# Another PSUM bank for the second token tile's inner values, and output products two steps behind

## The chip, the cores and the metric

The kernel runs on one core of one Trainium2 chip. The time is that of one execution on the device, in microseconds (us). Three runs of the kernel before took 954.71 to 959.58 us, with a median of 956.01.

## The reference

Inputs are q, k and v of 4 batches, 8 heads, 576 positions and 64 values, and two pairs of weights, 512 x 2048 and 2048 x 512. Everything is float32.

```
scores = q k^T / 8 - slope[h] * |i - j|       where 0 <= i - j < 128, else -1e9
x   = softmax(scores) v                        (2304 tokens x 512)
h   = x @ w_in;   g = h * clip(h + 3, 0, 6) / 6;   x = g @ w_out       (layer 1)
h   = x @ w_in2;  g = s * relu(h)^2 + b;           out = g @ w_out2    (layer 2)
```

## The kernel before, in words

**Precision.** Each float32 factor is split into a high half (rounded to fp32r) and a low half (the rest), and a product is made of three matmuls: high x high, high x low, low x high. So x, g and the weights all exist as two halves.

**Tiles and steps.** Layer 1 has eight token tiles (t = 0 to 7): four of 256 tokens, then four of 320. Layer 2 has six of 384 tokens (t = 8 to 13). The 2048 inner values are 16 blocks f of 128. A step (t, f) consists of: an inner product `h` (L563, 12 matmuls into one PSUM bank), `relu` on ScalarE (ACT, L580), `product` on VectorE (DVE, L586), `hi` on ACT, which writes the high half of g (L596), `lo` on DVE, which writes the low half (L605), and an output product `o` on TensorE (PE, L615), which adds the block's share to the tile's output banks. In layer 1 the product reads the PSUM bank of h again; in layer 2 only relu reads it. After a tile's last step, `end` (L651) copies the output banks out, in turn on ACT and DVE, and stores them: layer 1 to a buffer in DRAM, `x2d`, from which layer 2 loads its input, layer 2 to the output. Tile 7 writes its result into one SBUF buffer `whole` (L655) with the tag that x of tile 7 had before, and two transfers on SyncE (SP) take it from there.

**Order.** The whole program is written out by hand. Each piece of work is put into a numbered slot with a rank (`at`, L69), and the slots are emitted in order, within a slot by rank. Each engine runs its own instructions strictly in that order. A step i of the list `steps` has h in slot 14 + 2i (one earlier for t = 2 to 6), relu and product in the same slot, hi and lo in the next, and o in the slot `oslot + 1`. With the `oslot` of L82, PE's order is h of step i+1, o of step i, h of step i+2, o of step i+1. In the list the steps of tiles 0 and 1 alternate, tile 1 four blocks behind; the other tiles come one after another.

**What else runs beside the steps.** Until about 140 us the weights of layer 1 are split, two halves per block (`Half`, L141): ACT writes a scaled copy z into a PSUM bank and scales the raw words (L177, L178), DVE puts sign and exponent together (L182, L185), POOL adds (L191), ACT writes the high half (L199), and DVE the low half (L203). From tile 7 to the last block of tile 8 the weights of layer 2 are split in the same way; their z lies in the PSUM bank of tag "h". Attention of the token tiles 2 to 7 (`Unit`, L238) runs beside the steps too, one unit of one head every four slots: scores s (PE, L319), minima on DVE (L335, L336), exponentials on ACT (L346), weights on POOL (L362), transposes t (PE, L371), a copy F on ACT (L375), masks on POOL (L387), values v (PE, L402).

**Banks.** PSUM has eight banks. Four (tags o0 to o3) hold outputs. One, of tag "h", holds h of tiles 0 to 6. Three, of tag "a", rotate: s, t, v and the z of layer 1 take them (`bank`, L128), and from tile 7 on h does. A tile with a tag gets the buffer of that tag that has been free longest in program order, and its first instruction waits for the last reader of the tile that had it.

**SBUF buffers of the change.** The late pool has two buffers each of the tags "t" (the activation) and "g" (both halves of g).

Of the kernel before, what the change touches and what calls it, by code (L numbers as in the profile page):

```python
# [9 lines left out]
F32R = mybir.dt.float32r  # L10
# [6 lines left out]
P = 128  # L17
# [5 lines left out]
def tile_alibi_window_attention_moe_moe2(  # L23
# [17 lines left out]
    NF = w1.shape[0]  # L41
# [12 lines left out]
    xpool = ctx.enter_context(tc.tile_pool(name="xpool", bufs=1))  # L54
# [6 lines left out]
    nt1 = len(SIZES1)  # L61
# [10 lines left out]
    FIRST = 14  # L72
# [6 lines left out]
    hslot, oslot = {}, {}  # L79
    for i, tf in enumerate(steps):  # L80
        hslot[tf] = FIRST + 2 * i - 1
        oslot[tf] = FIRST + 2 * i + 2  # L82

# [11 lines left out]
    own = const.tile([P, P], I32, name="own")  # L97
# [43 lines left out]
    class Half:  # L141
# [51 lines left out]
        def hi(self):  # L193
            if (self.layer, self.f) not in wt:
                wt[self.layer, self.f] = wpool.tile(
                    [P, 2, 2 * DM], F32R, tag=f"w{self.f}", name=f"w{self.layer}_{self.f}"
                )
            w = wt[self.layer, self.f]
            nc.scalar.activation(w[:, 0, self.c], self.l.bitcast(F32), AF.Copy)  # L199
# [11 lines left out]
    xtag = ["x0", "x1", "x2"] + [f"x{(i + 1) % 2}" for i in range(3, nt1)]  # L211
    N2R = SIZES1[2]

    def x_tile(i):
        if i not in xt:
            n = N2R if xtag[i] == "x2" else N1
            xt[i] = xpool.tile([P, CC, 2, n], F32R, tag=xtag[i], name=f"x{i}")
            xt[i] = xt[i][:, :, :, : SIZES1[i]]
        return xt[i]
# [18 lines left out]
    class Unit:  # L238


        def __init__(self, g, b, qa, qb, h):
            self.g, self.b, self.qa, self.qb, self.h = g, b, qa, qb, h
            self.ka = max(0, qa - 1)
            self.nq = min(qb * P, S) - qa * P
            self.nk = min(qb * P, S) - self.ka * P
            self.nkb = qb - self.ka
            self.id = f"{b}_{qa}_{h}"
# [173 lines left out]
    class StartUnit(Unit):  # L421
# [111 lines left out]
    raws = {}  # L533
    units = [
        (StartUnit if i < NATIVE else Unit)(i, *g, h)
        for i, g in enumerate(groups)
        for h in range(H)
# [5 lines left out]
    class Step:  # L543
# [19 lines left out]
        def h(self):  # L563
            w = wt[self.layer, self.f]
            x = x_tile(self.t) if self.layer == 1 else xt[self.t]
            tag = dict(tag="h") if self.t < nt1 - 1 else dict(tag="a", bufs=3)
            self.ps = ps_w.tile([P, 512], F32, name=f"h{self.t}_{self.f}", **tag)[:, : self.n]
            m = 0
            for cc in range(CC):
                for wp, xp in ((0, 0), (0, 1), (1, 0)):  # L570
                    nc.tensor.matmul(  # L571
                        self.ps,
                        lhsT=w[:, wp, cc * P : (cc + 1) * P],
                        rhs=x[:, cc, xp],
                        start=m == 0,
                        stop=m == 3 * CC - 1,
                    )
                    m += 1
# [16 lines left out]

        def hi(self):  # L596
            pool, n = (gpool, N1) if self.layer == 1 else (late["p"], N2)
            self.g = pool.tile([P, 2, n], F32R, tag="g", name=f"g{self.t}_{self.f}")
            self.g = self.g[:, :, : self.n]
            if self.layer == 1:  # L600
                nc.scalar.activation(self.g[:, 0], self.a, AF.Copy)  # L601
            else:
                nc.scalar.activation(self.g[:, 0], self.a, AF.Identity, bias=b_sb)  # L603

        def lo(self):  # L605
            hi = self.g[:, 0].bitcast(F32)
            if self.layer == 1:
                nc.vector.tensor_tensor(out=self.g[:, 1], in0=self.a, in1=hi, op=ALU.subtract)  # L608
            else:
                nc.vector.scalar_tensor_tensor(  # L610
                    out=self.g[:, 1], in0=self.a, scalar=b_sb, in1=hi,
                    op0=ALU.add, op1=ALU.subtract,
                )
# [106 lines left out]
    for k in range(2 * NF):  # L720
        f, i = divmod(k, 2)
# [83 lines left out]
```

## Time and profile before

| | |
|---|---|
| median of three runs | 956.01 us (954.71 to 959.58) |
| the profiled execution, its own time | 958.67 us |
| its span, first to last instruction | 956.9 us |
| TensorE busy | 938.5 us, 98% |
| VectorE busy | 532.3 us, 56% |
| ScalarE busy | 465.9 us, 49% |
| GpSimd busy | 270.4 us, 28% |
| DMA, read and written | 63.44 MB and 9.44 MB |
| mean granted clock of TensorE | 0.985 |

The profile is one execution. Busy time counts the instructions of an engine, and a matmul's end is modelled, so a full PE row does not say that PE is at its peak. PEld is TensorE's weight load, which overlaps the matmuls. In a timeline each row is one instruction or a run of equal ones (x12 is twelve): start, duration, engine, line, operation, what it writes and reads, the shapes, and in brackets the idle time of the engine before it with the engine that released it. A row of the waits names who waited for whom: us in total, how often, the longest.

### The profile page before, as it was taken

Reading aid. Unit: us, or ns where it says so; the run is one execution under the profiler, and the core shown is the slowest. Engines: PE = TensorE matmul, PEld = TensorE weight load, DVE = VectorE, ACT = ScalarE, POOL = GpSimd, SP = SyncE. Lnnn points to the kernel's source line nnn. Section 1 sums busy time; section 2 is a strip of 40 time slices with the busy share of each in tenths; the row PEclk is TensorE's granted clock in tenths of the full one; section 3 lists DMA queues with packets and bytes.
Section 4 is the critical chain, followed back from the end, with each engine's and each line's share of the span. In section 5 each row is a group of like instructions: output and inputs, shape, how many; then the busy total and the mean of one; then the engine's idle time right before and its main releaser. Section 6 shows DMA issues by size and latency. Waiting matters only on the chain.

```text
span 956.9 us, 16309 instructions
## 1 busy us (share of the span) xinstructions
PE 938.5 (98%) x5978; PEld 865.6 (90%) x5978; DVE 532.3 (56%) x1334; ACT 465.9 (49%) x1201; POOL 270.4 (28%) x544
## 2 busy tenths in 40 slices
PE   8998999999999999999999999999999999999998
PEld 5688889999999999999999888799999999999997
DVE  5999885555555555455359999733333323323322
ACT  4988885455554545454347767523223223323322
POOL 5535773345544444434104533100000000000000
PEclk7699999999999999999999999999999999999999
DMA  7244632223221121220046455010200200200000
GB/s 286 89 160 140 206 114 75 81 73 105 67 95 61 49 96 61 73 72 17 1 144 193 142 182 165 13 54 1 66 1 1 66 1 1 66 1 0 34 1 34
DMA packets 34383, 73.92 MB, mean 77 GB/s; under 512 B 4352, under 2 KB 13568, under 8 KB 34304
## 3 DMA queue, kind: packets, MB, share of 16 engines
q1 hardware_dynamic: 34304, 72.89, 23.2%
q8 instruction: 47, 0.77, 0.3%
q14 instruction: 32, 0.26, 0.1%
HBM read 63.44 MB, written 9.44 MB: 76 GB/s over the span
## 4 chain that ended last, share of the span: by engine, by line
PE 78%; DVE 9%; ACT 4%; DMA 3%; issue 3%; POOL 1%; SPq 0%; ACTq 0%; POOLq 0%; DVEq 0%
PE h L571 34%; PE o L643 18%; PE o L629 16%; PE s L319 3%; PE v L402 3%; DMA raw<-w 2%; DVE w L203 2%; DVE z L182 2%; PE t L371 2%; PE s L474 2%; ACT z L177 1%; DVE t L592 1%; DVE raw L185 1%; PE t L513 1%; ACT w L199 1%
## 5 line engine op out<-in xcount | busy, mean ns | idle before, releaser
L571 PE MATMUL h<-x,w 128*128 128x384 f32 (+2 forms) x2688 | 445.9, 315 | 4.3 <-DVE t L588 4.2
L571 PEld LDWEIGHTS h<-x,w 128*128 128x128 f32 x2688 | 417.6, 189 | 15.1 <-DVE t L588 6.3
L584 ACT ACTIVATE t<-h 128x384 f32<-128x384 f32 (+2 forms) x224 | 99.5, 444 | 366.7 <-PE h L571 366.6
L629 PE MATMUL o<-g,w 128*128 128x256 f32 (+1 forms) x1536 | 230.4, 299 | 1.7 <-DVE g L608 1.2
L643 PE MATMUL o<-w,g 128*128 128x512 f32 x864 | 216.8, 395 | 3.5 <-ACT g L603 2.0
L629 PEld LDWEIGHTS o<-g,w 128*128 128x128 f32 x1536 | 210.0, 189 | 3.8 <-DVE g L608 1.9
L643 PEld LDWEIGHTS o<-w,g 128*128 128x128 f32 x864 | 159.9, 188 | 36.3 <-ACT g L603 4.5
L592 DVE SCALAR_TENSOR_TENSOR t<-t,s_sb 128x384 f32<-128x384 f32 x96 | 63.1, 658 | 171.5 <-ACT t L584 171.5
L387 POOL TENSOR_SCALAR_AFFINE_SELECT W<-F 128x128 f32<-128x128 f32 (+1 forms) x240 | 68.0, 320 | 148.9 <-ACT F L375 148.8
L588 DVE SCALAR_TENSOR_TENSOR t<-t,h 128x256 f32<-128x256 f32 (+1 forms) x128 | 57.7, 451 | 83.6 <-ACT t L584 83.6
L610 DVE SCALAR_TENSOR_TENSOR g<-t,b_sb,g 128x384 fp32r<-128x384 f32 x96 | 63.7, 663 | 54.1 <-ACT g L603 54.0
L608 DVE TENSOR_TENSOR g<-t,g 128x256 fp32r<-128x256 f32 (+1 forms) x128 | 70.5, 551 | 40.2 <-ACT g L601 39.4
L603 ACT ACTIVATE g<-t,b_sb 128x384 fp32r<-128x384 f32 x96 | 59.2, 617 | 63.6 <-DVE t L592 63.6
L191 POOL TENSOR_TENSOR raw<-raw 128x512 int32<-128x512 int32 x47 | 54.5, 1159 | 106.8 <-DVE raw L185 44.4
L601 ACT ACTIVATE g<-t 128x256 fp32r<-128x256 f32 (+1 forms) x128 | 56.0, 437 | 16.1 <-DVE t L588 16.1
L300 POOL TENSOR_TENSOR C<-raw,C 64x448 fp32r<-64x448 f32 (+1 forms) x48 | 51.0, 1062 | 36.2 <-issue 22.5
L362 POOL TENSOR_SCALAR P<-P,st 128x128 f32<-128x128 f32 x128 | 53.0, 427 | 7.1 <-DVE st L356 5.6
L346 ACT ACTIVATE P<-P,st 128x128 f32<-128x128 f32 x128 | 49.6, 391 | 0.0
L335 DVE COPY_PREDICATED s<-own,s 128x128 f32<-128x128 int32 (+1 forms) x112 | 30.8, 275 | 33.0 <-PE s L319 31.2
L182 DVE TENSOR_SCALAR z<-z 128x512 int32<-128x512 int32 x64 | 44.1, 689 | 1.1 <-ACT z L177 0.7
L203 DVE TENSOR_TENSOR w<-raw,w 128x512 fp32r<-128x512 f32 x47 | 42.6, 907 | 0.0
L336 DVE CUSTOM_DVE_ANT_0 P<-s,rel 128x128 f32<-128x128 f32 x128 | 37.2, 290 | 7.3
(73 smaller groups left out, 778.5 us busy)
## 6 DMA issues: line engine op xcount, KB each, us to landing
raw<-w SPq DMA_DIRECT2D x47, 512.0 KB, 4.3
raw<-qk SPq DMA_DIRECT2D x32, 384.0 KB, 3.0
stage<-w SPq DMA_DIRECT2D x17, 512.0 KB, 5.3
out<-y SPq DMA_DIRECT2D x18, 256.0 KB, 2.3
raw<-qk SPq DMA_DIRECT2D x16, 256.0 KB, 2.6
rv<-v SPq DMA_DIRECT2D x16, 256.0 KB, 3.3
raw<-qkv0p SPq DMA_DIRECT2D x8, 384.0 KB, 7.2
x2d<-y SPq DMA_DIRECT2D x8, 320.0 KB, 2.7
```

What stands on the lines that cost most here:

```text
L182: nc.vector.tensor_scalar(out=z, in0=z, scalar1=3, scalar2=None, op0=ALU.logical_shift_left)
L203: nc.vector.tensor_tensor(out=w[:, 1, self.c], in0=self.l.bitcast(F32), in1=w[:, 0, self.c].bitcast(F32), op=ALU.subtract,)
L387: nc.gpsimd.affine_select(out=self.W[:, o : o + r], in_=self.F[:, q : q + r], fill=0.0, base=k - 1, compare_op=ALU.is_ge, pattern=[[s, r]] ...
L571: nc.tensor.matmul(self.ps, lhsT=w[:, wp, cc * P : (cc + 1) * P], rhs=x[:, cc, xp], start=m == 0, stop=m == 3 * CC - 1,)
L584: nc.scalar.activation(self.a, self.ps, AF.Relu, **bias)
L588: nc.vector.scalar_tensor_tensor(out=self.a, in0=self.a, scalar=6.0, in1=self.ps, op0=ALU.min, op1=ALU.mult)
L592: nc.vector.scalar_tensor_tensor(out=self.a, in0=self.a, scalar=s_sb, in1=self.a, op0=ALU.mult, op1=ALU.mult)
L603: nc.scalar.activation(self.g[:, 0], self.a, AF.Identity, bias=b_sb)
L608: nc.vector.tensor_tensor(out=self.g[:, 1], in0=self.a, in1=hi, op=ALU.subtract)
L610: nc.vector.scalar_tensor_tensor(out=self.g[:, 1], in0=self.a, scalar=b_sb, in1=hi, op0=ALU.add, op1=ALU.subtract,)
L629: nc.tensor.matmul(acc[t][d], lhsT=w[:, wp, DM + d * P : DM + (d + 1) * P], rhs=self.g[:, gp], start=f == 0 and i == 0 and (t > 1 or d % 2 ...
L643: nc.tensor.matmul(acc[t][tb], lhsT=self.g[:, gp, tb * P : (tb + 1) * P], rhs=w[:, wp, DM:], start=f == 0 and i == 0, stop=f == NF - 1 and ...
```

## The change

Three edits. In `Step.h` the inner values of tile 1 take a bank of tag "a" in place of the bank "h". In the list of slots the o of layer 2 comes two slots later, so that PE's order there is h of step i+2, o of step i, h of step i+3, o of step i+1. At the boundary o of tile 7's last step stays where it is, and h of two more steps of tile 8 comes before the first o of tile 8. As a step's g now lives longer, `Step.hi` gives each third g of layer 2, beginning with the first of tile 8, a place in the buffer that held `whole`, the result of tile 7.

```diff
-        oslot[tf] = FIRST + 2 * i + 2
+        oslot[tf] = FIRST + 2 * i + (2 if tf[0] < nt1 else 4)
...
-            tag = dict(tag="h") if self.t < nt1 - 1 else dict(tag="a", bufs=3)
+            own = self.t != 1 and self.t < nt1 - 1
+            tag = dict(tag="h") if own else dict(tag="a", bufs=3)
...
-            self.g = pool.tile([P, 2, n], F32R, tag="g", name=f"g{self.t}_{self.f}")
+            tag = "g"
+            if self.layer == 2 and (self.t * NF + self.f) % 3 == 2:
+                pool, tag = xpool, xtag[nt1 - 1]
+            self.g = pool.tile([P, 2, n], F32R, tag=tag, name=f"g{self.t}_{self.f}")
```

## Rows read from the trace of the kernel before

**Rows 1.** Page, first part: busy us, share of the span, instructions.
```profile
PE 938.5 (98%) x5978; PEld 865.6 (90%) x5978; DVE 532.3 (56%) x1334; ACT 465.9 (49%) x1201; POOL 270.4 (28%) x544
```
**Rows 2.** Waits of PE in the whole span: us, times, longest.
```profile
PE h L571 <- DVE t L588: 4.2, 8, 1.3
```
**Rows 3.** Busy time by stretch: length, each engine's busy time, PEclk, DMA, GB/s.
```profile
72.00:96.00 24.00, 21.52 (x169) 20.11 (x168) 23.28 (x55) 20.36 (x50) 13.62 (x17) 1.00 0.49 144
...
549.00:612.00 63.00, 60.05 (x82) 1.00 0.40 132
```
**Rows 4.** Timeline of PE in layer 2, one step and the next h.
```profile
858.63 2.27 PE L571 MATMUL h<-x,w 128*128 128x384 f32 x12
860.74 2.24 PE L643 MATMUL o<-w,g 128*128 128x512 f32 x9
862.82 2.27 PE L571 MATMUL h<-x,w 128*128 128x384 f32 x12
```
**Rows 5.** Timeline of PE while tiles 0 and 1 alternate.
```profile
87.83 1.70 PE L571 MATMUL h<-x,w 128*128 128x256 f32 x12 [1.26 <-DVE t L588]
...
99.34 1.60 PE L571 MATMUL h<-x,w 128*128 128x256 f32 x12
100.78 0.24 PE L319 MATMUL s<-C,qX 128*128 128x128 f32 x1
...
101.25 1.59 PE L629 MATMUL o<-g,w 128*128 128x256 f32 x12
103.42 1.70 PE L571 MATMUL h<-x,w 128*128 128x256 f32 x12 [0.57 <-DVE t L588]
...
109.22 0.23 PE L319 MATMUL s<-C,qX 128*128 128x128 f32 x1
...
114.53 1.60 PE L571 MATMUL h<-x,w 128*128 128x256 f32 x12
...
119.00 1.70 PE L571 MATMUL h<-x,w 128*128 128x256 f32 x12 [0.58 <-DVE t L588]
```
**Rows 6.** Timelines of ACT and DVE there: readers of rotating banks.
```profile
100.22 0.36 ACT L375 ACTIVATE F<-t 128x256 f32<-128x256 f32 x1
...
109.56 0.69 DVE L185 SCALAR_TENSOR_TENSOR raw<-raw,z 128x512 int32<-128x512 int32 x1
...
113.89 0.64 ACT L177 ACTIVATE z<-raw 128x512 f32<-128x512 f32 x1 [0.69 <-DMA raw<-w]
...
115.80 0.36 ACT L375 ACTIVATE F<-t 128x256 f32<-128x256 f32 x1
```
**Rows 7.** Timelines of ACT, DVE and PE at the start of layer 2.
```profile
548.57 0.62 ACT L603 ACTIVATE g<-t,b_sb 128x384 fp32r<-128x384 f32 x1
...
550.58 0.98 DVE L610 SCALAR_TENSOR_TENSOR g<-t,b_sb,g 128x384 fp32r<-128x384 f32 x1
...
549.24 0.50 PE L643 MATMUL o<-w,g 128*128 128x512 f32 x1
```
**Rows 8.** Timeline of SP, and the landing of line 667's two transfers there.
```profile
550.34 0.81 SPq L667 DMA_DIRECT2D x2d<-y  x2
...
DMA to landing us min/median/max: 2.2/3.0/3.7
```
**Rows 9.** Timelines of DVE and PE, and waits from 543 to 612 us.
```profile
610.30 1.53 DVE L203 TENSOR_TENSOR w<-raw,w 128x512 fp32r<-128x512 f32 x1
...
611.41 2.48 PE L571 MATMUL h<-x,w 128*128 128x384 f32 x12
...
DVE g L610 <- ACT g L603: 2.3, 4, 0.7
...
PEld h L571 <- DVE w L203: 0.3, 1, 0.3
```
**Rows 10.** Timeline of PE's weight loads at the last output product.
```profile
951.42 1.48 PEld L643 LDWEIGHTS o<-w,g 128*128 128x128 f32 x7 [0.36 <-DVE g L610]
```
**Rows 11.** Line 610 from 551 to 612 us: duration in ns, min/median/max.
```profile
L610 DVE SCALAR_TENSOR_TENSOR g<-t,b_sb,g x14: 607/620/1400, 550.6 to 609.8; 128x384 fp32r<-128x384 f32 x14
```

## The prediction

> **What bounds the kernel now.** I read four views in this order. The page's first part: TensorE (PE) is busy for 98% of the span, VectorE (DVE) for 56% [rows 1]. That is a mean over stages, so next the waits: PE stands before an inner product for 4.2 us in eight places, always behind DVE's product, the last reader of the one bank that the first two token tiles share [rows 2]. Then the busy time by stretch: from 72 to 96 us DVE is busy for 23.28 of 24 us, and from 549 to 612 for 60.05 of 63 [rows 3]. In these stretches DVE splits the weights besides its share of the steps, and PE's gaps follow from that. Last the timelines of the two places that the change touches [rows 5 to 9]. Elsewhere PE sets the pace: in the second layer a step is an inner product (h) of 860.74 - 858.63 = 2.11 us and an output product (o) of 862.82 - 860.74 = 2.08 [rows 4].
>
> What the reader should keep: where DVE is full, giving PE room ahead buys nothing unless DVE itself gets faster.
>
> **Part 1: tile 1's h in the rotating banks.** It removes the waits on the shared bank and adds the 16 h of tile 1 to three banks that attention (s, t, v) and weight splitting (z) already use. PE instructions, shapes and order stay the same.
>
> *What goes.* The 4.2 us of [rows 2]. Three of the eight places come after 100 us, 0.57 and twice 0.58 (103.42, 119.00 and the same 15 us later) [rows 5]; so 2.5 us lie before 90 us, the largest 1.26 at 87.83 [rows 5], where DVE has 24 - 23.28 = 0.7 us in 24 to spare [rows 3]. A PE that arrives earlier only stands at the next thing that DVE's work releases: the transposes of attention wait for POOL's weights, which wait for DVE, and that wait grows by what the earlier one loses. Of this stretch I take 0.5 us as gained, as relu and the z copies reach DVE sooner; its ends are 0 and 2.5.
>
> *What comes.* Banks go round in the order in which they fall free in program order. With h of tile 1 put into that order, each tile's start in the trace can be held against the end of the last reader of the bank that it would get. Up to 99 us each is free, or all but free. Then five places are not:
> - h at 99.34 gets the bank whose transposes are copied out at 100.22 + 0.36 = 100.58: 1.24 us late [rows 5, 6].
> - s at 109.22 gets the bank of a z whose last DVE operation ends at 109.56 + 0.69 = 110.25: 1.03 late [rows 5, 6].
> - h at 114.53 gets the bank copied out at 115.80 + 0.36 = 116.16: 1.63 late [rows 5, 6].
> - The last two places come once more 15 us later, the same pattern.
>
> These 1.24 + 2 x (1.03 + 1.63), some 6.6 us, don't add up on the path, because waits that PE has now are eaten by them. Queued behind a waiting h or s on PE are the o of the step before and the next h; ACT's relu waits for them. Step by step: h of 99.34 starts at 100.6, s and o follow, and the h that now starts at 103.42 after 0.57 us of waiting [rows 5] needs no bank any more and starts at 100.6 + 1.44 (h) + 0.47 (s) + 1.44 (o, as h) = 104.0: 0.6 late [rows 5]. ACT gets its relu 0.6 late, so z and its end are too: s of 109.22 starts at 110.9, and all behind it is 1.6 late. The copy at 115.80 comes 1.0 late (ACT has 0.69 of waiting for a load to lose [rows 6]), h of 114.53 starts at 117.2, and the h of 119.00, rid of its 0.58 us of waiting, at 120.6: 1.6 late. So the pair of units costs 1.0 beyond the 0.6, and the next pair 1.0 more: 2.6 us. After 140 us the z are over and PE sets the pace, so a shift stays. Part 1: 2.6 - 0.5 = +2.1. From below: all 4.2 gone and no new wait, -4.2. From above: the full 6.6.
>
> **Part 2: o two steps behind.** A step's o now comes after h of the next two steps. One h is merely moved before each o, so no instruction comes or goes; three g tiles are needed, and each third lies in the space of the buffer that held the last layer-1 result (y of tile 7).
>
> *A new wait at the start.* (8*16 + 0) % 3 is 2: the very first g of the layer is the one in y's space. It can't be written before both transfers of y to DRAM have landed. Now ACT writes that g at 548.57. When DVE has finished y, the two transfers are issued from 550.34 on for 0.81 us and take 2.2 and 3.7 us to land [rows 8]; I take the second as the longer: about 550.75 + 3.7 = 554.45. So g's first half ends at 554.45 + 0.61, and DVE's second half, at 550.58 now [rows 7], starts at 555.1: 4.5 us late, less 0.36 as it then runs beside no POOL work (0.98 against a median of 0.62 [rows 7, 11]): 4.2. Queued behind on ACT: a weight half, the relu of the next step, z; behind on DVE: everything. SP's transfers aren't behind it. With a landing as fast as the first, 2.2 us, it would be 2.7.
>
> *Where does this land on the path?* From 551 to 612 DVE's queue is full: 3 us of 63 idle [rows 3], 2.3 of it the way from product over ACT to the second half inside one step [rows 9], none of it a wait for PE. So a late DVE stays late until the last weight half. Its split for h of step 15 runs 610.30 to 611.83, and h of that step, at 611.41, already waits for it (0.3 us) [rows 9]. After the change it is ready at 611.83 + 4.2 = 616.0. PE's own work allows 607.5: o of step 0 from 555.1 on, then 12 h of 2.11 and 13 o of 2.08. So DVE decides, and PE stands for 8 us in between. The granted clock is 1.00 throughout now [rows 3]; should it fall in the gap of 4 us, PE has those 8 us in hand.
>
> *What is left behind it.* Before, o of step 13 precedes h of step 15; now only o of step 12 does. So one o, 2.08 us, moves from the time in which PE waited for DVE to the time after it. This is so even without the new wait: room for PE to run ahead makes the order of what it can do worse, as h waits for weights and o is the work that could fill the gap.
>
> *What goes.* From 549.24 [rows 7] to 611.41 [rows 9] are 62.2 us for 14 o and 13 h, 29.1 + 27.4 = 56.5: 5.7 us of PE waiting for g. They vanish as waits for g and come back as waits for weights, as above. At the very end the last o no longer stands behind its g: 951.42 shows 0.36 on the weight loads [rows 10]; I take 0.3 off. Part 2: 4.2 + 2.1 - 0.3 = +6.0. From below: no late landing and half of DVE's 3 us of idle time won back, 2.1 - 1.5 - 0.3 = +0.3; or the whole 5.7 gone, if DVE didn't bind, -6. From above: a landing 1 us later, +7. Switches between the tiles of layer 2 show no gap now and keep the same h between two tiles' o.
>
> **Sum.** +2.1 + 6.0 = +8.1 us. The profiled execution took 958.67 us (span 956.9) and would take 966.8. The median of the runs is 956.01, 2.7 below; with it 964.1. I forecast 964.
>
> **Rivals.**
> *A, the shift is made up: 958.* DVE loses time to POOL: a second half of g takes 0.62 us in the median of 14 and up to 1.40 [rows 11], the long ones where they start beside POOL's add. If the 4.2 us of shift takes five such apart, at 0.78 each, DVE is back in time: then part 2 is 2.1 - 0.3, and with part 1 at nothing 956.0 + 1.8 = 957.8. Against: POOL's add is released by DVE's own operation before, so it falls on the same place. The Trainium skill's SBUF — State Buffer (Who interferes with whom) says that the two engines share a port pair, that a DVE instruction with two SBUF inputs meets a POOL one that reads SBUF there, and that the later one is blocked wholly; the trace agrees, with 0.78 us of blocking; were it gone for good, DVE would be A's.
>
> *B, the other side, faster: 946.* Between 551 and 612 PE stops for g; with a second step of room it doesn't stop, and relu reaches ACT and DVE sooner, so that the weights too come sooner. Then 4.2 + 5.7 + 0.3 go, 956.0 - 10.2 = 946. The point from which it decides is whether DVE's full stretch ends before 607.5, when PE's own work reaches h of step 15. For it: the gaps lie exactly where the change gives room. Against: DVE has 3 us idle there, none of it from PE. The Trainium skill's Perfetto Trace Analysis (Optimization Strategy) has the rule on this side: gaps that repeat can mean that there are too few buffers for the next tile; by it the time is B's. Here the gaps stand on an engine that waits for a full one.
>
> *C, more: 970.* The bank waits do add up, since a z without a bank holds the relu behind it on ACT and so takes away the slack that eats them: 956.0 + 6.6 + 7.
>
> *D, only the order of o counts:* no late landing on the path, part 1 as forecast: 956.0 + 2.1 + 1.8 = 959.9.
>
> **How the numbers follow.** Forecast 0.58 (its own range 960 to 968), A 0.13, D 0.14, B 0.08, C 0.07. 0.5% of 956 is 4.8 us, about what a measurement of this kernel can tell from no change; faster means under 951.2, slower over 960.8. Faster is B: 0.08. Same is A and D: 0.27. Slower is the forecast and C: 0.65. The range reaches to A and C and leaves out B and what lies beyond these two: 957 to 970.
>
> **What would show it.** Right, if in the profile after: (1) ACT's first second-layer g starts near 554 behind a transfer, and PE shows one gap of about 4 us there; (2) DVE stays full to about 616, and PE's gaps before that stand on DVE's weight halves at h (few do now); (3) the waits of h for DVE's product before 140 us are gone, and h and s wait for ACT's copy and DVE's sign operation, over a us each, from 99 us on; (4) tile 2 starts about 2 us later. The prediction is wrong if DVE's stretch ends by 612, if the first g doesn't wait, or if the first 160 us come out shorter.

## The result and the profile after

The changed kernel takes 969.68 us (median of 4 runs, 968.26 to 971.32), the one before 957.8 in the runs beside it: a ratio of 1.0115, 95% interval 1.0082 to 1.0148, so 11.0 us more (7.9 to 14.2; the two medians lie 11.9 apart). The profiled execution took 969.79 us with a span of 968.1, which is 11.2 above the span of before.

The first part of the page shows as much work as [rows 1], in a longer span (busy us, share, instructions):

```profile
PE 941.2 (97%) x5978; PEld 870.6 (90%) x5978; DVE 533.0 (55%) x1334; ACT 465.8 (48%) x1201; POOL 267.6 (28%) x544
```

PE has the same 5978 matmuls and yet 2.7 us more busy time: some of them ran slower. Where the time went is best read by holding the start of each inner product against its start in the kernel before. That is a subtraction of two PE timelines, worked out here for after and for four of the experiments below (us, positive is later; "(t, f)" is token tile and step):

| start of h | after | part 1 alone | part 2 alone | part 2, third g in y's space | the same, gaps filled |
|---|---|---|---|---|---|
| (0, 0) | +0.69 | -1.06 | +0.68 | -0.12 | -0.89 |
| (1, 4), about 92 us | +1.87 | -1.34 | +0.66 | +0.45 | -0.94 |
| (1, 11), about 145 us | +4.31 | +1.76 | +1.46 | +0.18 | -1.59 |
| (7, 15), about 540 us | +4.28 | +1.73 | +1.45 | +0.17 | -1.62 |
| (8, 15), about 611 us | +6.09 | +1.71 | +3.22 | -1.52 | -3.27 |
| (13, 15), about 947 us | +9.27 | +1.75 | +6.20 | +2.87 | -1.63 |
| span | +11.2 | +1.8 | +7.9 | +4.6 | +0.1 |

Three things are to be seen. From 145 to 540 us the numbers stand still, in all of them: there PE sets the pace. Before that they drift even where layer 1 is as it was: by +0.8, +0.3 and -0.7 us from (0, 0) to (1, 11) in the last three columns, and by +1.3 and +3.0 in two runs further down, the second of which began 6.7 us early. So a shift of less than about 1 us in the first 145 us needn't come from a change. And where part 2 is in, the span grows by some 1.7 us more than the last h: the o of 2.08 that is left over at the end, less 0.3 or so of the old tail.

**The first 160 us.** PE's own waits between 36 and 160 us, the three largest sums (us, times, longest):

```profile
PE h L572 <- ACT F L375: 3.1, 3, 1.0
PE s L319 <- DVE raw L185: 2.2, 3, 0.9
PE t L371 <- POOL P L362: 2.1, 2, 1.7
```

The 4.2 us of h behind DVE's product [rows 2] are gone from this list (0.5 us is left, at 61 us, for tile 0). In their place h waits for ACT's copy F of a transpose, and s for the DVE operation that ends the life of a z. The places, on PE's timeline:

```profile
101.77 1.69 PE L572 MATMUL h<-x,w 128*128 128x256 f32 x12 [1.04 <-ACT F L375]
...
112.04 0.30 PE L319 MATMUL s<-C,qX 128*128 128x128 f32 x1 [0.85 <-DVE raw L185]
...
118.30 1.69 PE L572 MATMUL h<-x,w 128*128 128x256 f32 x12 [1.04 <-ACT F L375]
```

These are the h of 99.34, the s of 109.22 and the h of 114.53 in [rows 5], now 2.4, 2.8 and 3.8 us later. Three shorter waits for a z's DVE operation are new too: s at 78.22 and at 85.18 us, 0.52 each, and h at 142.89, 0.44. And PE is already 1.87 us late before the first of the three rows, at (1, 4); 0.69 of that was there at the first h. At (1, 3), 83 us, it was 0.09 late, so 0.6 had been won; then 1.8 were lost at a place that the prediction named for its wait, but not for the clock. After, and then the same two transposes before:

```profile
87.14 1.60 PE L572 MATMUL h<-x,w 128*128 128x256 f32 x12
90.44 0.33 PE L371 MATMUL t<-ident,P 128*128 128x128 f32 x1 [1.70 <-POOL P L362]
91.21 0.48 PE L371 MATMUL t<-ident,P 128*128 128x128 f32 x1 [0.45 <-POOL P L362]
91.34 2.91 PE L633 MATMUL o<-g,w 128*128 128x256 f32 x12
94.05 1.70 PE L572 MATMUL h<-x,w 128*128 128x256 f32 x12
```

```profile
89.80 0.33 PE L371 MATMUL t<-ident,P 128*128 128x128 f32 x1 [0.27 <-POOL P L362]
90.57 0.33 PE L371 MATMUL t<-ident,P 128*128 128x128 f32 x1 [0.45 <-POOL P L362]
```

Before, h of 87.83 waited 1.26 us for DVE [rows 5] and the transposes 0.27 and 0.45. Now h is early, and the transposes behind it wait 1.70 and 0.45 us for POOL's weights. The o after them takes 2.91 us, at a granted clock of 0.50 from 91 to 93 us; an o of this shape takes 1.59 [rows 5].

**The start of layer 2.** Timeline of all engines from 553.5 us:

```profile
554.63 0.80 SPq L671 DMA_DIRECT2D x2d<-y  x2
...
558.04 0.61 ACT L607 ACTIVATE g<-t,b_sb 128x384 fp32r<-128x384 f32 x1 [5.20 <-DMA x2d<-y]
...
558.68 0.62 DVE L614 SCALAR_TENSOR_TENSOR g<-t,b_sb,g 128x384 fp32r<-128x384 f32 x1 [3.73 <-ACT g L607]
558.70 3.79 PE L647 MATMUL o<-w,g 128*128 128x512 f32 x9 [3.17 <-ACT g L607]
```

The first g waits for y's two transfers, as forecast. Against [rows 7] DVE's second half is 558.68 - 550.58 = 8.10 us late; 4.31 of that came with it from the first 160 us, so 3.8 are new; as the operation takes 0.62 us now and took 0.98, 3.4 are left behind it. PE's gap there is 3.17 us, and its first o takes 3.79 instead of 2.24 us [rows 4]. In the stretches by time (length, busy time of PE, PEld, DVE, ACT and POOL, granted clock, DMA share, GB/s) the clock falls behind that gap, and once more after 616 us:

```profile
553.00:560.00 7.00, 3.83 (x18) 3.32 (x17) 3.23 (x7) 1.96 (x4) 1.04 (x1) 0.89 0.49 170
560.00:563.00 3.00, 3.00 (x11) 2.43 (x11) 2.97 (x5) 3.00 (x7) 0.97 (x1) 0.68 0.52 171
...
616.00:626.00 10.00, 7.03 (x27) 6.27 (x28) 6.48 (x10) 3.97 (x7) 1.19 (x1) 0.83 0.00 0
```

**The end of DVE's full stretch.** DVE's split for h of step (8, 15), then PE's timeline from 611 us:

```profile
618.00 1.53 DVE L203 TENSOR_TENSOR w<-raw,w 128x512 fp32r<-128x512 f32 x1
```

```profile
611.20 2.03 PE L572 MATMUL h<-x,w 128*128 128x384 f32 x10 [1.42 <-DVE w L203]
613.07 2.25 PE L647 MATMUL o<-w,g 128*128 128x512 f32 x9
617.49 0.61 PE L572 MATMUL h<-x,w 128*128 128x384 f32 x2 [2.17 <-ACT w L199]
619.58 3.30 PE L572 MATMUL h<-x,w 128*128 128x384 f32 x10 [1.47 <-DVE w L203]
622.67 2.56 PE L647 MATMUL o<-w,g 128*128 128x512 f32 x9
625.07 2.27 PE L572 MATMUL h<-x,w 128*128 128x384 f32 x12
```

DVE's operation starts 7.70 us later than in [rows 9], 3.4 beyond the 4.31. PE has done all it may do and stands before h's first and third matmul. Behind these two gaps ten matmuls of h take 3.30 us (2.03 in the step before, the first row) and o 2.56 (2.25): 1.6 us lost to the slow clock (a mean of 0.83 from 616 to 626 us, in the stretches above), with nothing in hand.

### The profile page after: what moved, and what is told of

It is laid out like the page before. It is cut to its first block, busy times and chain, and to the rows that moved or that the text cites. A ratio compares the mean times of both kernels' runs of the same rounds, so it can differ in the third digit from the quotient of the medians.

```text
span 968.1 us, 16322 instructions
## 1 busy us (share of the span) xinstructions
PE 941.2 (97%) x5978; PEld 870.6 (90%) x5978; DVE 533.0 (55%) x1334; ACT 465.8 (48%) x1201; POOL 267.6 (28%) x544
## 4 chain that ended last, share of the span: by engine, by line
PE 80%; DVE 10%; ACT 4%; issue 3%; DMA 1%; POOL 0%; SPq 0%; ACTq 0%; POOLq 0%; DVEq 0%
PE h L572 35%; PE o L647 18%; PE o L633 17%; PE s L319 3%; DVE w L203 3%; PE v L402 2%; DVE z L182 2%; PE s L474 2%; PE t L371 2%; DVE raw L185 1%; DVE t L593 1%; ACT z L177 1%; PE t L513 1%; DVE g L612 1%; DVE t L589 1%
## 5 line engine op out<-in xcount | busy, mean ns | idle before, releaser
L647 PEld LDWEIGHTS o<-w,g 128*128 128x128 f32 x864 | 162.1, 189 | 34.2 <-ACT g L607 4.5
L362 POOL TENSOR_SCALAR P<-P,st 128x128 f32<-128x128 f32 x128 | 50.6, 410 | 7.0 <-DVE st L356 5.5
```

The costliest lines, as they stand in the source:

```text
L647: nc.tensor.matmul(acc[t][tb], lhsT=self.g[:, gp, tb * P : (tb + 1) * P], rhs=w[:, wp, DM:], start=f == 0 and i == 0, stop=f == NF - 1 and ...
```

## The experiments

In all of them the kernel before ran on the same chip. A difference in us is the ratio of the times, less 1, by some 959 us. Two parts, and what hangs on each, come first; then the causes in part 2; last the early steps of part 1.

### Part 1 alone

```
-            tag = dict(tag="h") if self.t < nt1 - 1 else dict(tag="a", bufs=3)
+            own = self.t != 1 and self.t < nt1 - 1
+            tag = dict(tag="h") if own else dict(tag="a", bufs=3)
```

> Part 1 alone: h of tile 1 in the rotating banks, layer 2 as before. Theory (bank waits, plus a slow clock behind one gap): 2.4 us of waits of h and s for z and transposes from 99 to 135 us, and 1.2 us because the granted clock falls behind the 1.7 us gap at the transposes near 90 us: +3 to +4.5 us. Rival (what the first 160 us showed is mostly chance between executions, 0.7 us of it was there before the first h): -1 to +1 us.

Measured: 962.79 us, ratio 1.0037 (1.0013 to 1.0060), +3.5 us: in the theory's range, and the rival's +1 is outside the interval. Of the theory's two terms the first is larger in this trace and the second is not there, as will be seen. From 99 us on h and s wait over 0.8 us at the five places worked out in the prediction:

```profile
99.21 1.69 PE L572 MATMUL h<-x,w 128*128 128x256 f32 x12 [1.27 <-ACT F L375]
109.49 0.30 PE L319 MATMUL s<-C,qX 128*128 128x128 f32 x1 [0.85 <-DVE raw L185]
115.75 1.70 PE L572 MATMUL h<-x,w 128*128 128x256 f32 x12 [1.04 <-ACT F L375]
126.02 0.30 PE L319 MATMUL s<-C,qX 128*128 128x128 f32 x1 [0.86 <-DVE raw L185]
132.28 1.70 PE L572 MATMUL h<-x,w 128*128 128x256 f32 x12 [1.04 <-ACT F L375]
```

They sum to 5.1 us, but from (1, 4) to (1, 11) PE loses 3.1 (table; 2.4 in after): waits that were there before are eaten, as the prediction said. Three shorter waits for a z are here as in after (s at 76.48 and 83.44 us, h at 140.34; 0.53, 0.51 and 0.44). At the transposes near 88 us PE waits 1.45 and 0.45 us, and the o behind them takes 1.67 us, at a granted clock of 1.00:

```profile
88.46 0.33 PE L371 MATMUL t<-ident,P 128*128 128x128 f32 x1 [1.45 <-POOL P L362]
89.24 0.33 PE L371 MATMUL t<-ident,P 128*128 128x128 f32 x1 [0.45 <-POOL P L362]
89.32 1.67 PE L630 MATMUL o<-g,w 128*128 128x256 f32 x12
```

Up to layer 2 this kernel and after are the same program. So the slow clock there belongs to an execution of it, and the theory's 1.2 us for it isn't shown as a cost of part 1.

### Part 2 alone

```
-        oslot[tf] = FIRST + 2 * i + 2
+        oslot[tf] = FIRST + 2 * i + (2 if tf[0] < nt1 else 4)
...
+            if self.layer == 2 and (self.t * NF + self.f) % 3 == 2:
+                pool, tag = xpool, xtag[nt1 - 1]
```

> Part 2 alone: o of layer 2 two steps behind, first g in the place of y, h of tile 1 as before. Theory (DVE sets the pace to the last weight half): 3.4 us from the late first g, 2.1 us for the o that moves behind the stretch, 1.6 us of slow clock: +6 to +8 us. Rival (the two parts need each other): +3 us or less.

Measured: 966.87 us, 1.0087 (1.0058 to 1.0115), +8.3, a little above the theory's range, which lies within the interval. The rival is out. With part 1's 3.5 that makes 11.8, against 11.0 for both: within their intervals the parts add up.

### The wait taken away: the third g in y's space

```
-            if self.layer == 2 and (self.t * NF + self.f) % 3 == 2:
+            if self.layer == 2 and (self.t * NF + self.f) % 3 == 1:
```

> Part 2 without the late first g: the third g of layer 2 instead of the first goes where y lay, o two steps behind, h of tile 1 as before. Theory (DVE's stretch isn't shortened by room for PE, and one o moves behind it): +2 to +4 us, the upper end if the granted clock falls in the gaps before h of step 15. Rival (the landing is the whole loss, and without it the room pays): -3 to -6 us.

By this edit the first g in y's space is that of step (8, 2), the third of the layer; some expectations below call it the second. Measured: 963.37 us, 1.0037 (1.0014 to 1.0059), +3.5. So room without the late first g is still a loss. By the times the late g is worth 4.8 of part 2's 8.3 us, but the two intervals leave 1.3 to 8.3. By the traces taking it away wins some 2 us: from (7, 15) to (13, 15) PE loses 4.75 with it and 2.70 without (table), since 3.4 of lateness go and the slow clock below costs more. From (8, 3) to (8, 14) h starts 3.4 to 5.4 us earlier than before, 2.1 of it only because one o fewer stands in front. DVE is not ahead, its last split starts at 610.41 (610.30 in [rows 9]), and the lead is gone at h of step 15:

```profile
609.89 0.62 PE L571 MATMUL h<-x,w 128*128 128x384 f32 x2 [2.17 <-ACT w L199]
611.99 3.57 PE L571 MATMUL h<-x,w 128*128 128x384 f32 x10 [1.49 <-DVE w L203]
615.36 3.49 PE L646 MATMUL o<-w,g 128*128 128x512 f32 x9
618.69 2.26 PE L571 MATMUL h<-x,w 128*128 128x384 f32 x12
```

```profile
606.00:611.00 5.00, 2.34 (x10) 1.37 (x8) 4.94 (x7) 3.53 (x7) 2.07 (x2) 1.00 0.00 0
611.00:616.00 5.00, 4.01 (x12) 3.91 (x13) 2.69 (x4) 1.62 (x3) 0.39 (x1) 0.52 0.00 0
```

PE is busy for 2.34 of 5 us from 606 to 611, and then the granted clock is 0.52: h takes 3.57 instead of 2.03 us, o 3.49 instead of 2.24. Together that looks like 1.54 + 1.25 = 2.8 us of slow clock; the run with filled gaps, below, tests it.

### Only the place of the first g

o one step behind, as before; the first g of each three in y's space.

```
+            if self.layer == 2 and (self.t * NF + self.f) % 3 == 2:
+                pool, tag = xpool, xtag[nt1 - 1]
```

> The late first g alone: each third g where y lay, beginning with the first of layer 2, but o one step behind as before, and h of tile 1 as before. Theory (what DVE loses at the start of layer 2 it doesn't make up until the last weight half): +3.5 to +5.5 us. Rival (DVE makes it up in 15 steps, or it is only the landing in front of the deeper order that costs): -0.5 to +1 us.

Measured: 964.90 us, 1.0051 (1.0030 to 1.0071), +4.9, as the theory has it. The wait alone costs this much without the new order. Within its trace it costs more, 6.7 us from (7, 15) to (8, 15). 3.5 are the late g; 2.8 more come at 558.73, where DVE stands for a product (and 0.3 at the next), since ACT's relu stood behind an h at half clock (0.50 from 551 to 556 us):

```profile
550.26 0.61 ACT L606 ACTIVATE g<-t,b_sb 128x384 fp32r<-128x384 f32 x1 [5.21 <-DMA x2d<-y]
...
550.93 4.21 PE L646 MATMUL o<-w,g 128*128 128x512 f32 x9 [5.24 <-ACT g L606]
...
554.93 3.18 PE L571 MATMUL h<-x,w 128*128 128x384 f32 x12
...
558.21 0.49 ACT L584 ACTIVATE t<-h 128x384 f32<-128x384 f32 x1 [4.20 <-PE h L571]
558.73 0.62 DVE L592 SCALAR_TENSOR_TENSOR t<-t,s_sb 128x384 f32<-128x384 f32 x1 [2.80 <-ACT t L584]
```

Two steps behind, the h of the next step is done before the late o, and this second wait does not arise.

### PE's two gaps filled

To the kernel with the third g in y's space, in front of the first and the third matmul of h (8, 15):

```
+                    if late15 and m in (0, 2):
+                        for _ in range(12 if m == 0 else 9):
+                            nc.tensor.matmul(
+                                fill, lhsT=wt[2, 0][:, 0, :P], rhs=x[:, 0, 0],
...
```

> The kernel with part 2 alone and its second g (not the first) in y's space, plus work for PE that no output uses: 12 matmuls of 384 columns (about 1.9 us at full clock) before h of step (8, 15), which PE waits 2.2 us for, and 9 more (1.4 us) in front of its third matmul, which it waits 1.5 us for. Each lies in a gap that is there already. Theory (part of the loss is TensorE's clock, granted at 0.5 for some 5 us behind these two gaps, where h took 3.57 for 2.03 us and o 3.49 for 2.1): the clock stays up and the run takes 2 to 3 us less than the kernel without the filling, so some 0 to +1.5 us against before. Rival 1 (h and o are slow there because their weights come piecewise): no difference, +3.5 us. Rival 2 (the filling is late itself and only queues in front): +0.5 to +1.5 us more than without it.

Measured: 960.79 us, 1.0008 (0.9991 to 1.0025), +0.8: 2.7 less than without the filling, as the theory has it; the +3.5 of rival 1 is outside the interval. The traces say 2.7 as well: from (7, 15) to (13, 15) PE loses nothing here and 2.70 without. DVE and ACT release h as before; only PE is busy meanwhile:

```profile
608.13 0.62 PE L580 MATMUL h<-x,w 128*128 128x384 f32 x2
608.59 1.73 PE L576 MATMUL fill<-x,w 128*128 128x384 f32 x9
610.23 2.03 PE L580 MATMUL h<-x,w 128*128 128x384 f32 x10
612.10 2.24 PE L655 MATMUL o<-w,g 128*128 128x512 f32 x9
```

```profile
611.00:616.00 5.00, 5.00 (x28) 4.61 (x27) 2.16 (x4) 1.47 (x3) 0.00 (x0) 1.00 0.00 0
```

h takes 2.03 us, o 2.24, the clock is 1.00. From (7, 15) to (13, 15) the table's last column doesn't move (-1.62, -1.63), so what is left of part 2 is the o at the end: 2.08 less 0.3.

### DVE relieved: the input split on POOL

To the kernel before:

```
-            eng = nc.gpsimd if self.t == nt1 else nc.vector
+            eng = nc.gpsimd
```

> The kernel before, with the input split of the second layer's later tiles (four subtractions of 128x384 a tile, 0.76 us each on DVE) on POOL. In DVE's full stretch from 551 to 612 us these are 4, 3.05 us of 60. Theory (DVE's own queue paces this stretch, PE's gaps in it are only a shadow): DVE ends its last weight half 2 to 3 us earlier, and the run takes 1 to 3 us less than before. Rival (PE's gaps there come from the one step of room for g, so from the order, not from DVE's load): no difference, -0.5 to +0.5; if POOL's splits hold DVE up through the shared SBUF port, up to +1.5.

Measured: 957.54 us, 0.9983 (0.9962 to 1.0003), -1.6, at the edge of what can be told. In the trace it can be told: the shift of PE against before is -0.40 at (7, 15) and -1.43 at (8, 15), and stays, so 1.0 us comes out of DVE's stretch. DVE's split for step 15 starts there at 608.89, 1.4 before [rows 9], not the 2 to 3 us expected, and less than the 3.05 us of work taken off. The trace shows where the rest went, and it is what the expectation names beside its rival: between the first g's second half and that split DVE's 14 products take 13.2 us instead of 11.7 and its 14 second halves 13.7 instead of 12.9. Each long one, some 1.4 us in place of 0.6, runs beside a POOL operation, one product and one second half beside the split itself and the others beside POOL's add.

The same on top of the order with the third g in y's space:

> Part 2 alone with its second g in y's space, and the input split of the later tiles on POOL, as in the run beside it. Theory (room ahead pays only as far as DVE gets faster): DVE's last half is done 2 to 3 us earlier, h of step (8, 15) too, and since PE's gap there shrinks to about half, the clock may stay up (2.7 us more): 2 to 5.5 us less than without it, so -2 to +1.5 us against before. Rival (the loss of this order does not hang on DVE): it stays +3 to +4 us.

Measured: 960.95 us, 1.0012 (0.9993 to 1.0030), +1.2, so 2.3 less than without, a difference that the two intervals don't hold clear of 0. The size fits, half of the reason doesn't. Within the trace only 1.0 us is won from (7, 15) on, and the gap didn't shrink: PE no longer waits at step 14, so what it waits comes in one piece at step 15, and the clock falls again (0.65 and 0.58 from 611 to 620 us):

```profile
611.13 0.62 PE L571 MATMUL h<-x,w 128*128 128x384 f32 x2 [2.78 <-ACT w L199]
613.23 3.57 PE L571 MATMUL h<-x,w 128*128 128x384 f32 x10 [1.48 <-DVE w L203]
616.59 3.51 PE L646 MATMUL o<-w,g 128*128 128x512 f32 x9
```

Both at once, POOL's split and filling (15 and 9 matmuls):

> Part 2 alone with its second g in y's space, the input split on POOL, and filling for PE that no output uses (15 matmuls before h of step (8, 15), 9 before its third). Without filling, this kernel's clock still fell to 0.5 behind that gap and it measured +1.2 us; with filling but without the split on POOL it was +0.8. Theory (two separate terms: DVE's load, worth 1 to 1.6 us, and the slow clock, worth 2.7): -1.5 to 0 us against before. Rival (the split on POOL only paid by keeping PE's gap short, so that both runs won the same thing): +0.5 to +1.5.

Measured: 960.33 us, 1.0016 (0.9994 to 1.0038), +1.5. The median speaks for the rival; the interval reaches to the theory's 0. In its trace the clock is 1.00 and PE goes from +0.42 at (7, 15) to -0.64 at the end: 1.06 us better than with filling alone. So the trace has the two terms side by side, and the times don't resolve one of 1 us.

### Two steps behind, but only after DVE's stretch

To the kernel with the third g in y's space:

```
-        oslot[tf] = FIRST + 2 * i + (2 if tf[0] < nt1 else 4)
+        oslot[tf] = FIRST + 2 * i + (2 if tf[0] <= nt1 else 4)
```

> Part 2's order (o two steps behind, three g) only from the layer's second tile on, that is from about 620 us, after DVE's full stretch; in the first tile o stays one step behind. Theory (the moved o and the gap cost only because DVE is full there; elsewhere PE is full and order is free): within 0.5 us of before. Rival (o two steps behind costs by itself, by one o left over at the end of the kernel or by switching accumulators): +2 us or more, as one o takes 2.08.

Measured: 959.97 us, 1.0009 (0.9988 to 1.0031), +0.9: the interval holds both. The trace decides: PE is 1.86 us late at (7, 15), 1.87 at (8, 15), and 0.24 early from (9, 3) on, with one o of 2.08 more behind it. So it ends 2.08 - 0.24 - 0.3 = 1.5 us late, no later than it came. Moving o costs nothing where PE is full.

### Part 1 for the early steps only

```
+            own = self.t < nt1 - 1 and not (self.t == 1 and self.f < 5)
+            tag = dict(tag="h") if own else dict(tag="a", bufs=3)
```

> Part 1 for h of steps (1, 0) to (1, 4) alone, which start before 99 us; later h of tile 1 have their own bank again. Theory (part 1's loss comes from the five places from 99 us on, where the bank that comes round still has a reader; before that the banks are free and a little is gained): -1 to 0 us against before, and in its profile no wait of h for ACT's copy out of a transposes' bank, while h's three waits of 0.57 us for DVE's product after 100 us are back. Rival (the loss starts earlier: the h in the rotating banks holds up attention near 88 us, where PE's clock fell behind the waits for POOL): +1 to +2 us.

Measured: 955.88 us, 0.9986 (0.9961 to 1.0011), -1.3: just beyond the theory's range and within noise of it, with most of the rival's range outside. Within its trace PE wins 0.5 from (0, 0) to (1, 11), no more than the drift there. In PE's waits none is left for ACT's F at h, and four for DVE's product are there, 2.2 us. The two waits near 89 us are 1.46 and 0.45 us here, and the clock stays at 1.00. So part 1's loss lies in the places from 99 us on. With POOL's split as well:

> The same, with the input split of the second layer's later tiles on POOL as well (alone it measured -1.6 us). The two places lie 450 us apart and share no queue then, so the effects should add up: -1 to -3 us against before, under both kernels. Rival (either effect is within the noise of executions): -0.5 to +0.5.

Measured: 958.56 us, 1.0000 (0.9980 to 1.0019). This missed. In the trace POOL's split is worth its 1.0 us again (-4.36 at (7, 15), -5.40 at (8, 15)), but the runs scatter by more. And near 85 us, where the program is still that of the run before it, the same waits of 1.46 and 0.45 us have a slow clock behind them this time: 0.53 from 86 to 89 us, 2.61 us for the o, and 1.2 us lost between (1, 3) and (1, 4). None of these kernels is measurably faster than the one before.

## Why the prediction was right, and 5.7 us too low

It said slower, with 964 as the time, and its three losses are there: banks, the late first g, the o left behind. 969.68 lies just inside the upper end of the whole range, 970, but outside the forecast's own, 960 to 968. That upper end came from rival C, bank waits that add up to 6.6 us, and the runs have them at 2.4 and 3.1; so that the time is inside is in part luck. Of the 5.7 us, 1.8 are the base (957.8 in the runs beside it, 956.01 in those shown). 3.1 are the terms below, 11.2 us between the two profiles against the 8.1 forecast, and the last 0.8 is that the medians lie a little further apart than the profiles. Its signs came as well: the first g stood behind a transfer, DVE was busy past 616 us, h and s waited for ACT's copy and DVE's operation; only tile 2 started 4.3 us later instead of 2.

- **Bank waits from 99 us on: +2.6 forecast, 2.4 in after, 3.1 in part 1 alone.** Right in cause and size, and in the five large places. Not right was that before 99 us each bank is free or all but free: s waits 0.52 us for one at 78.22 and again at 85.18, and h 0.44 at 142.89. The early steps, run by themselves, cost nothing.
- **A gain of 0.5 before 90 us: not found in after.** 0.6 was won up to (1, 3), but from (0, 0) to (1, 4) PE lost 1.2 us. The reason given was right, that a PE that comes earlier stands at the next thing that DVE's work releases; what was missed is that two waits then become one of 1.70 us, behind which the clock fell: 2.91 us for an o of 1.59. This isn't a fixed cost of the change. Four profiles have the same program up to there: the clock fell in after (1.70 and 0.45 us) and in the early steps with POOL's split (1.46 and 0.45), and stayed in part 1 alone (1.45 and 0.45) and in the early steps alone (1.46 and 0.45), where 0.3 was gained by (1, 4). What decides between them is not shown.
- **The late first g: 4.2 forecast, 3.4 found.** Right in mechanism, a little large. I had DVE's half start 4.5 us late and win 0.36 back; it starts 3.8 late and takes 0.62 us instead of 0.98 [rows 7], which leaves 3.4, and these 3.4 are still there at the end of the stretch. The difference is the landing: I took 3.7 us, and the longest now was 2.9. Taking the wait away took 4.8 us off by the times (8.3 to 3.5) and some 2 by the traces, as more of the slow clock came in its place.
- **One o left behind the stretch: 2.1 forecast, 2.08 less 0.3 found,** by the filled run: all else put back, PE's lag there is nil and that o remains. Where PE is full, the same move is free.
- **The step that failed** is this one: "The granted clock is 1.00 throughout now [rows 3]; should it fall in the gap of 4 us, PE has those 8 us in hand." It held for the gap it spoke of: 0.68 from 560 to 563 us, and paid by waiting that was to come anyway. But those 8 us are themselves gaps, and the last of them stand at h of step 15, with nothing in hand behind. There the clock fell and cost 1.6 us in after, 2.7 with the third g, none once PE had something to do. I named that place and left its clock out.

In the trace: 2.4 + 1.2 + 3.4 + 1.6 + 2.1 - 0.2 = 10.5, and 0.7 of a later start, which belongs to the execution and not to the change, make the 11.2. The 1.2 hangs on whether the clock falls near 90 us, and the 2.4 is good to about 1 us, as the drift in the table shows.

Of the rivals, B had the gaps that go, and they did go; the Trainium skill's Perfetto Trace Analysis (Optimization Strategy) reads repeated gaps as a possible want of buffers. With a third g and no late landing h did start up to 5.4 us earlier (2.1 of it the moved o), and the kernel was 3.5 us slower: the gaps were a full DVE's shadow. Taking 3 us of work off DVE won 1.0 us with either order. Nothing speaks for A: behind that first operation DVE is 3.5 us late, and it is 3.4 late at its last split. C is nearest in time and wrong in reason: its bank waits don't add up. D was the rest of it: without the late g and the slow clock part 2 comes to its 1.8 (1.7 in the trace of the filled run).

## What to carry to other kernels

Room ahead of an engine that waits for a full one bought nothing here: it gathered many short waits into a few long ones, spent the work that could have filled them, and then the clock fell behind them. So when a forecast says "it stands for 8 us", ask where those 8 us stand, and price the work right behind each at half the clock, as the bad case, unless something is in hand there. Before giving a buffer a second use, look at who reads it last: here a transfer's landing of 2.9 us held up ACT, DVE and PE at once.

## What was unexpected of the hardware

**The clock can fall behind quite short gaps, and not in every execution.** Behind 1.70 and 0.45 us of waiting it was at 0.50 (after, 91 to 93 us), behind 2.17 and 1.49 us at 0.52 (third g in y's space). Behind 1.46 and 0.45 us it fell to 0.53 in one profile (early steps with POOL's split) and stayed at 1.00 in another of the same program up to there (early steps alone); 1.45 and 0.45 us (part 1 alone), or a single 1.26 [rows 5], left it at 1.00. So the length of the gaps alone doesn't decide it.

**Executions differ by their first 40 us.** Granted clock from 10 to 20 and from 20 to 40 us, in the profiles of before and of the kernel that only moves the first g; nothing that they do there differs:

```profile
10.00:20.00 10.00, 9.41 (x40) 5.48 (x37) 6.85 (x43) 7.68 (x31) 7.25 (x18) 0.69 1.03 408
20.00:40.00 20.00, 20.00 (x73) 12.31 (x74) 17.81 (x53) 15.92 (x46) 12.39 (x21) 0.50 0.34 119
```

```profile
10.00:20.00 10.00, 9.65 (x58) 5.88 (x54) 8.76 (x50) 9.25 (x37) 8.39 (x21) 1.00 1.03 407
20.00:40.00 20.00, 15.74 (x85) 10.34 (x85) 19.59 (x61) 18.45 (x53) 13.72 (x23) 0.91 0.42 146
```

The first h starts at 38.37 and 31.69 us, and of the 6.68 us by which the second is early, 3.50 are left at 540 us. Runs of one and the same kernel spread over up to 10 us (952.61 to 962.55 for the kernel before), and this is at least a part of it. So an effect of 1 us is read from shifts inside one trace, between two places behind the first 145 us, and not from the median of a dozen runs.
